# Local and global attention followed by a GELU feed-forward: the last batch's activations are written in output order, its tiles go out in one transfer each, and its last tile is moved to the end

## The chip, the cores and the metric

The kernel runs on one core of one Trainium2 chip. The metric is the device time of one execution in microseconds (us); the median of several runs is compared. The engines are called by the names of the profile: PE (TensorE matmuls; PEld is its weight load), DVE (VectorE), ACT (ScalarE), POOL (GpSimd) and SP (SyncE, which here only issues transfers).

## The reference

The inputs are queries, keys and values for 8 batches with 8 heads of dimension 64: 512 local and 32 global tokens each. Global tokens attend to everything; a local token attends to the global tokens and to the local ones within a window of 32. The result is laid out as tokens by 512 features and goes through a feed-forward of width 2048:

```python
s_g = scale * np.matmul(q_g, k_all.transpose(0, 1, 3, 2))
out_g = np.matmul(sm(s_g), v_all)
mask = np.abs(pos[:, None] - pos[None, :]) <= window      # window = 32
s_l = np.concatenate([s_lg, s_ll], axis=-1)               # s_ll is -1e9 outside the mask
out_l = np.matmul(sm(s_l), np.concatenate([v_g, v_l], axis=2))
x = concat(out_g, out_l): (8 * 544 tokens, 512)
h = x @ w_in                                              # 512 x 2048
g = h * (1.0 / (1.0 + np.exp(-1.702 * h)))
return (g @ w_out).astype(np.float32)                     # 2048 x 512, out is 4352 x 512
```

In the output, the rows of one batch are its 32 global tokens followed by its 512 local ones.

## The kernel before, in words

All matmuls take bf16 operands and accumulate in fp32. The order of the instructions on each engine is the order in which the program writes them; the program interleaves the stages by hand.

The attention works on groups of four heads. It leaves, for each batch, a tile xL of 512 features (four blocks of 128 partitions) by 512 local tokens, and one common tile xG with the 8 x 32 = 256 global tokens. In xL the local tokens are not in output order: token number 16 r + t stands in column 32 t + r (t from 0 to 15, r from 0 to 31). This comes from the way in which queries and keys are loaded, and runs through all later stages.

The feed-forward has two phases for each batch i from 0 to 7, and for i = 8, which the program calls B and which is the set of 256 global tokens:

- The **h phase** has 16 steps, one for each block fc of 128 of the 2048 inner features. `h_step` (L623) takes a PSUM bank hp, does four accumulating matmuls with `h_mm` (L612), and calls `h_act`: a Tanh on ACT from hp into a tile th (L619) and one DVE instruction `(th + 1) * hp` into `gTs[i][:, fc]` in bf16 (L620). A batch has 512 columns, the global tokens have 256. There are four th buffers.
- The **o phase** has one tile `tci` for every 128 tokens: four tiles in a batch, two for the global tokens. `o_mm` (L630) does a quarter of a tile, four accumulating matmuls of 512 columns with gT as the weights (L637); at the fourth quarter `o_out` copies the PSUM bank to the tile ob on ACT with a factor of 0.5 (L651) and issues the output transfers (L659). There are six ob buffers.

hp and op come from one pool of four PSUM banks ("p"), so a new step waits until an earlier one has been read.

A tile of 128 columns holds four values of t, with 32 values of r each. So one output tile of a batch is written by four transfers of 32 rows, and the rows of each lie 16 rows apart in the output. For the global tokens each of the four transfers writes the 32 rows of one batch. All go through SP's queue, apart from the last tile.

The very last tile (`last` in `o_out`; in the kernel before the second tile of the global tokens) is split in its columns, 320 and 192: the 16 matmuls of the first part (L649), the copy and four transfers, then the same for the second part. Its transfers alternate between SP and ACT.

At the end of the program the h phase of the global tokens is interleaved with the o phase of batch 7: one h step, then one quarter of a tile, 16 times. Then come the first tile of the global tokens and the split last tile:

```python
for st in range(FC):
    h_step(B, st)
    o_mm(B - 1, st)
for st in range(4):
    o_mm(B, st)
o_out(B, 1, None)
```

Of the kernel before, what the change touches and what calls it, by code (L numbers as in the profile page):

```python
# [16 lines left out]
ALU = mybir.AluOpType  # L17
# [3 lines left out]
def kernel(  # L21
# [12 lines left out]
    nc = tc.nc  # L34

    B, H, Sl, D = q_l.shape
    Sg = q_g.shape[2]
    S = Sg + Sl
# [123 lines left out]
    for j in range(4):  # L162
        r = (j + 1) % 4
        nc.gpsimd.memset(bd[32 * r : 32 * r + 32, j, :], 1.0)
    for i in range(2):
# [3 lines left out]
        out=step, in_=step, pattern=[[1, 289]], compare_op=ALU.is_ge,  # L169
# [108 lines left out]
    def pbank(name):  # L278
        return psP.tile([128, 512], F32, name=name, tag="p")
# [323 lines left out]
    gTs, ops = {}, {}  # L603

    def width(i):
        return TB if i < B else B * Sg
# [9 lines left out]
    def h_act(i, fc, hp):  # L616
        n = width(i)
        th = moe.tile([128, TB], F32, name="th", bufs=4)
        nc.scalar.activation(th[:, :n], hp[:, :n], AF.Tanh, scale=0.851)  # L619
        nc.vector.scalar_tensor_tensor(gTs[i][:, fc, :n], in0=th[:, :n], scalar=1.0,  # L620
                                       in1=hp[:, :n], op0=ALU.add, op1=ALU.mult)

    def h_step(i, fc):  # L623
        if fc == 0:
            gTs[i] = moe.tile([128, FC, TB], BF16, name="gT")
        hp = pbank("hp")
        h_mm(i, fc, hp, range(NKC))
        h_act(i, fc, hp)

    def o_mm(i, st):  # L630
        tci, f4 = divmod(st, 4)
        first = (i, tci) not in ops
        if first:
            ops[i, tci] = pbank("op")
        op = ops[i, tci]
        for fc in range(4 * f4, 4 * f4 + 4):
            nc.tensor.matmul(op, lhsT=gTs[i][:, fc, tci * 128 : tci * 128 + 128],  # L637
                             rhs=w_out_sb[:, fc, :], start=(first and fc == 4 * f4), stop=(fc == FC - 1))
        if f4 == 3:
            o_out(i, tci, op)  # L640

    def o_out(i, tci, op):
        ob = moe.tile([128, d_model], F32, name="ob", bufs=6)
        last = i == B and tci == B // 4 - 1
        for lo, hi in ((0, 320), (320, 512)) if last else ((0, 512),):
            if last:
                op = pbank("op")
                for fc in range(FC):
                    nc.tensor.matmul(op[:, lo:hi], lhsT=gTs[i][:, fc, tci * 128 : tci * 128 + 128],  # L649
                                     rhs=w_out_sb[:, fc, lo:hi], start=(fc == 0), stop=(fc == FC - 1))  # L650
            nc.scalar.activation(ob[:, lo:hi], op[:, lo:hi], AF.Copy, scale=0.5)  # L651
            for j in range(4):
                eng = nc.scalar if last and j % 2 else nc.sync
                if i < B:
                    rows = out[i * S + Sg : (i + 1) * S, :].rearrange("(r t) m -> t r m", t=16)[4 * tci + j]
                else:
                    r = (4 * tci + j) * S
                    rows = out[r : r + Sg, :]
                eng.dma_start(out=rows[:, lo:hi], in_=ob[32 * j : 32 * j + 32, lo:hi])  # L659

    def act4(i, hf):
        f = slice(2 * hf, 2 * hf + 2)
# [164 lines left out]
    for fc in range(FC):  # L827
        if fc < 4:
            h_act(1, fc, hps[fc])
        elif fc in (4, 6):  # L830
            f = slice(fc, fc + 2)
            th, ps = early[:, fc - 4 : fc - 2], pt[1 - (fc - 4) // 2]
            nc.scalar.activation(th, ps, AF.Tanh, scale=0.851)
            nc.vector.scalar_tensor_tensor(gTs[1][:, f, :], in0=th, scalar=1.0, in1=ps,
                                           op0=ALU.add, op1=ALU.mult)
        elif fc >= 8:
            h_step(1, fc)
        if fc < 4:
            a.ext((fc,), on_act)
        if fc == 10:  # L840
            a.S(0)
            a.X(0, (0,))
        if fc == 11:
            a.X(0, (1,))
            a.M(0, nc.gpsimd)
            load_v(3)
            load(4)
            load_g(8, NQ)
# [72 lines left out]
            phase_o(i)  # L921
    for st in range(FC):
        h_step(B, st)
        o_mm(B - 1, st)
    for st in range(4):
        o_mm(B, st)
    o_out(B, 1, None)


# [28 lines left out]
```

## Time and profile before

| | us |
|---|---|
| median of 3 runs | 299.13 (298.33 to 299.79) |
| profiled execution | 299.75 |
| its span in the profile | 298.0 |
| h phase of batch 7 on PE, about | 252.7 to 266.5 of the span |
| h phase of the global tokens with the o phase of batch 7 | 266.5 to 287.3 |
| last ACT copy (192 columns) | 294.51 to 294.84 |
| last transfers issued | 295.3 |

The profile is that of one execution. Busy times are for one engine; a line number (L620) is a line of the kernel before. Groups are listed as line, engine, operation, output and inputs, shape, count, then busy time in us and mean time of one in ns, then idle time of the engine ahead of them with what ended it. In the timeline a line has start and duration in us, engine, line and operation; several like instructions are merged into one line with their count. "Landing" of a transfer is the time from its issue to its completion.

### The profile page before, as it was taken

The numbers are of one execution on the slowest core, as the hardware profiler recorded it, in microseconds if no ns is written. First come the engines' busy times: TensorE is split into PE (matmuls) and PEld (weight loads), VectorE is DVE, ScalarE is ACT, GpSimd is POOL, SyncE is SP. The second block draws the span as 40 slices with busy tenths as digits, with TensorE's granted clock in tenths as the row PEclk, the third lists the DMA queues.
The fourth block names the chain that finished last, engine by engine and source line by source line (L and its number), as shares of the span: only waits on it lengthen the run. The fifth ranks groups of instructions, "written<-read, shape, count | busy, mean of one in ns | idle before, by whom it ended". The sixth has DMA issues, their size and how long they took to land.

```text
span 298.0 us, 8159 instructions
## 1 busy us (share of the span) xinstructions
PE 287.4 (96%) x3390; PEld 150.2 (50%) x3431; DVE 216.2 (73%) x422; ACT 173.6 (58%) x284; POOL 86.9 (29%) x136
## 2 busy tenths in 40 slices
PE   7999999998999999999999999999999999999995
PEld 6544445444454455445454455445544455445653
DVE  6768868887868878797979878787879766683220
ACT  4836867589347736577357654676547651663421
POOL 8973669639564002800072003500000000000000
PEclk9999999999999999999999999999999999999999
DMA  7999999998999312981199114901120022101113
GB/s 202 166 187 211 204 184 128 187 166 60 163 189 158 72 39 55 144 139 28 48 95 173 34 40 84 113 0 40 36 73 0 2 55 55 35 0 39 36 48 95
DMA packets 59541, 28.20 MB, mean 95 GB/s; under 512 B 47600, under 2 KB 49904, under 8 KB 59504
## 3 DMA queue, kind: packets, MB, share of 16 engines
q0 software_dynamic: 51664, 17.57, 53.5%
q1 hardware_dynamic: 7360, 9.45, 11.6%
q10 hardware_dynamic: 480, 0.66, 0.7%
q8 instruction: 27, 0.44, 0.7%
q14 instruction: 10, 0.08, 0.1%
HBM read 36.31 MB, written 8.91 MB: 152 GB/s over the span
## 4 chain that ended last, share of the span: by engine, by line
PE 86%; DVE 3%; ACT 2%; issue 2%; ACTq 0%; DVEq 0%
PE hp L612 36%; PE op L637 36%; PE s L557 5%; PE ov L583 5%; PE s L612 2%; ACT e L568 2%; ACT ob L651 1%; PE op L649 1%; DVE rs L463 1%; DVE sT L459 1%; DVE xL L468 1%; PE og L594 1%; DVE e L573 0%; PE ov L420 0%; PE ov L435 0%
## 5 line engine op out<-in xcount | busy, mean ns | idle before, releaser
L637 PE MATMUL op<-w_out_sb,gT 128*128 128x512 bf16 x498 | 119.1, 379 | 2.9 <-DVE rs L463 1.2
L620 DVE SCALAR_TENSOR_TENSOR gT<-th,hp 128x512 bf16<-128x512 f32 (+1 forms) x136 | 87.0, 655 | 35.7 <-ACT th L619 35.7
L612 PE MATMUL hp<-xL,w_in_sb 128*128 128x512 bf16 x471 | 104.8, 379 | 0.7 <-issue 0.2
L619 ACT ACTIVATE th<-hp 128x512 f32<-128x512 f32 (+1 forms) x136 | 77.7, 574 | 41.2 <-PE hp L612 38.5
L612 PEld LDWEIGHTS <-w_in_sb 128*128 128x128 bf16 x576 | 56.1, 98 | 64.3 <-issue 0.4
L637 PEld LDWEIGHTS <-gT 128*128 128x128 bf16 x528 | 49.4, 98 | 56.2 <-issue 1.3
L651 ACT ACTIVATE ob<-op 128x512 f32<-128x512 f32 (+2 forms) x35 | 20.5, 589 | 65.9 <-PE op L637 63.3
L97 POOL DMA_DIRECT2D v<-in_v_l_dram x40 | 30.9, 776 | 84.5 <-PE og L594 82.2
L568 ACT ACTIVATE e<-s 128x1016 bf16<-128x1016 f32 (+1 forms) x56 | 53.5, 1007 | 2.9 <-PE s L557 2.8
L573 DVE TENSOR_TENSOR e<-e,mask 128x1712 bf16<-128x1712 bf16 (+1 forms) x26 | 27.5, 1059 | 4.8 <-ACT e L568 4.3
L459 DVE STREAM_TRANSPOSE sT<-ov 128x512 f32<-128x512 f32 x15 | 10.8, 717 | 17.4 <-PE ov L583 15.9
L468 DVE TENSOR_TENSOR xL<-ov,rs 128x512 bf16<-128x512 f32 x29 | 18.7, 686 | 1.8 <-PE ov L435 0.5
L557 PEld LDWEIGHTS <-kT 32*128 32x128 bf16 x672 | 12.7, 93 | 12.5 <-issue 8.8
L509 DVE STREAM_TRANSPOSE kT<-rk 128x512 f32<-128x512 f32 x14 | 14.6, 1044 | 3.1 <-DMA rk<-in_k_l_dram 3.1
L557 PE MATMUL s<-q,kT 32*128 32x160 bf16 (+1 forms) x448 | 14.9, 246 | 0.0
L99 POOL DMA_DIRECT2D v<-in_v_g_dram x24 | 13.9, 581 | 0.2 <-issue 0.2
L463 DVE STREAM_TRANSPOSE rs<-rT 128x512 f32<-128x512 f32 x16 | 11.4, 711 | 0.6
L583 PE MATMUL ov<-e,v 128*32 128x128 bf16 (+3 forms) x624 | 11.7, 223 | 0.0
L314 DVE STREAM_TRANSPOSE q<-rq 128x512 f32<-128x512 f32 (+1 forms) x17 | 11.3, 665 | 0.2 <-ACT rq L675 0.2
L583 PEld LDWEIGHTS <-v 128*32 128x32 bf16 x672 | 10.5, 97 | 0.0
L612 PE MATMUL hp<-xG,w_in_sb 128*128 128x256 bf16 x64 | 9.6, 273 | 0.0
L557 PE MATMUL s<-qc,kT 32*128 32x120 bf16 (+1 forms) x224 | 8.0, 212 | 0.2 <-ACT e L568 0.2
(109 smaller groups left out, 182.4 us busy)
## 6 DMA issues: line engine op xcount, KB each, us to landing
out_dram<-ob SPq DMA_DIRECT2D x132, 64.0 KB, 2.3
rq<-in_q_l_dram POOLq DMA_DIRECT2D x5, 512.0 KB, 7.2
rk<-in_k_l_dram POOLq DMA_DIRECT2D x5, 512.0 KB, 9.9
v<-in_v_l_dram POOLq DMA_DIRECT2D x24, 96.0 KB, 4.2
w_in_sb<-in_moe_w_in_dram POOLq DMA_DIRECT2D x8, 256.0 KB, 7.8
w_out_sb<-in_moe_w_out_dram POOLq DMA_DIRECT2D x4, 512.0 KB, 10.3
rq<-in_q_l_dram POOLq DMA_DIRECT2D x5, 256.0 KB, 6.5
rk<-in_k_l_dram POOLq DMA_DIRECT2D x5, 256.0 KB, 7.7
```

The source lines that it names most:

```text
L97: nc.gpsimd.dma_start(out=vt[0:n, hs, c, :D], in_=vs[FIRST[c] : FIRST[c] + n, hs])
L468: nc.vector.tensor_mul(self.x[:, 2 * self.u + h, :], self.st[1 + h], self.st["rs"])
L509: nc.vector.transpose(flat[:, 0:Sl].rearrange("p (r t) -> p t r", t=16), loaded[self.b][0][:, self.u].bitcast(F32))
L557: nc.tensor.matmul(bank(self.ps, j)[:, at : at + n], lhsT=self.k[p, KEYS[c] : KEYS[c] + 128, e], rhs=qs[p, :, :, e], start=(e == 0), stop= ...
L568: nc.scalar.activation(self.E[rnd][:, 2 * i : 2 * i + 2, :n], self.ps[i][:, :, :n], AF.Exp, scale=scale)
L573: eng.tensor_mul(e, e, mask[:, rnd : rnd + 1, :n].to_broadcast([128, 4, n]))
L583: nc.tensor.matmul(ov[32 * j : 32 * j + 32, :].rearrange("p (t r) -> p t r", t=16)[:, t0:t1, r0 : r0 + nr], lhsT=lv, rhs=self.E[rnd][:, j, ...
L612: nc.tensor.matmul(hp[:, : width(i)], lhsT=w_in_c[:, fc // 4, kc, fc % 4 // 2, :, fc % 2], rhs=(xL[i] if i < B else xG)[:, kc, :], start=( ...
L619: nc.scalar.activation(th[:, :n], hp[:, :n], AF.Tanh, scale=0.851)
L620: nc.vector.scalar_tensor_tensor(gTs[i][:, fc, :n], in0=th[:, :n], scalar=1.0, in1=hp[:, :n], op0=ALU.add, op1=ALU.mult)
L637: nc.tensor.matmul(op, lhsT=gTs[i][:, fc, tci * 128 : tci * 128 + 128], rhs=w_out_sb[:, fc, :], start=(first and fc == 4 * f4), stop=(fc = ...
L651: nc.scalar.activation(ob[:, lo:hi], op[:, lo:hi], AF.Copy, scale=0.5)
```

## The change

Three things are changed, all of them for batch 7 and the end of the program.

First, `h_act` writes batch 7's gT in output order. Inputs th and hp are read in sequence as before; the output is addressed so that column 32 t + r of the input goes to column 16 r + t. Successive bf16 results therefore go 16 elements (32 bytes) apart.

Second, in `o_out` a tile of batch 7 now consists of 128 rows that follow each other in the output, and goes out in one transfer through SP instead of four. The global tokens keep four transfers a tile, all on SP.

Third, the order at the end: the first four h steps of the global tokens follow each other without an `o_mm`; the other twelve are each followed by one quarter of tiles 0, 1 and 2 of batch 7. Then come both tiles of the global tokens, unsplit, and at the very end the last tile of batch 7, split 320 and 192, with one transfer for each part.

```diff
@@ h_act
-        nc.vector.scalar_tensor_tensor(gTs[i][:, fc, :n], in0=th[:, :n], scalar=1.0,
-                                       in1=hp[:, :n], op0=ALU.add, op1=ALU.mult)
+        g, th, hp = gTs[i][:, fc, :n], th[:, :n], hp[:, :n]
+        if i == B - 1:
+            g = g.rearrange("p (r t) -> p t r", t=16)
+            th, hp = (v.rearrange("p (t r) -> p t r", t=16) for v in (th, hp))
+        nc.vector.scalar_tensor_tensor(g, in0=th, scalar=1.0, in1=hp, op0=ALU.add, op1=ALU.mult)
@@ o_out
-        last = i == B and tci == B // 4 - 1
+        last = i == B - 1 and tci == 3
...
             nc.scalar.activation(ob[:, lo:hi], op[:, lo:hi], AF.Copy, scale=0.5)
+            if i == B - 1:
+                r = i * S + Sg + 128 * tci
+                nc.sync.dma_start(out=out[r : r + 128, lo:hi], in_=ob[:, lo:hi])
+                continue
             for j in range(4):
-                eng = nc.scalar if last and j % 2 else nc.sync
...
-                eng.dma_start(out=rows[:, lo:hi], in_=ob[32 * j : 32 * j + 32, lo:hi])
+                nc.sync.dma_start(out=rows[:, lo:hi], in_=ob[32 * j : 32 * j + 32, lo:hi])
@@ the end
     for st in range(FC):
         h_step(B, st)
-        o_mm(B - 1, st)
-    for st in range(4):
+        if st >= 4:
+            o_mm(B - 1, st - 4)
+    for st in range(8):
         o_mm(B, st)
-    o_out(B, 1, None)
+    o_out(B - 1, 3, None)
```

## The prediction

> **What bounds the kernel now.** I read the page first, then the chain of waits at its end, then the timeline of the last 45 us, and last the groups of DVE instructions with their shapes kept apart. The page's first line:
>
> ```profile
> PE 287.4 (96%) x3390; PEld 150.2 (50%) x3431; DVE 216.2 (73%) x422; ACT 173.6 (58%) x284; POOL 86.9 (29%) x136
> ```
>
> TensorE is busy for 96% of the span and its granted clock is full in all 40 slices, so time is lost only where PE is made to stop, or behind its last matmul. The timeline of the stretch that the change touches:
>
> ```profile
> 254.40 0.69 DVE L620 SCALAR_TENSOR_TENSOR gT<-th,hp 128x512 bf16<-128x512 f32 x1 [2.98 <-ACT th L619]
> 254.65 12.03 PE L612 MATMUL hp<-xL,w_in_sb 128*128 128x512 bf16 x54
> ...
> 266.49 0.69 DVE L620 SCALAR_TENSOR_TENSOR gT<-th,hp 128x512 bf16<-128x512 f32 x1 [0.17 <-ACT th L619]
> 266.52 0.60 PE L612 MATMUL hp<-xG,w_in_sb 128*128 128x256 bf16 x4
> ...
> 267.35 1.02 DVE L620 SCALAR_TENSOR_TENSOR gT<-th,hp 128x512 bf16<-128x512 f32 x2 [0.18 <-ACT th L619]
> ```
>
> The h phase of batch 7 starts its 16 DVE instructions at 254.40 to 267.35, so one step lasts (267.35 - 254.40)/15 = 0.863 us, and that is PE's pace: each DVE instruction takes 0.69 us and then sits idle 0.17 us, waiting for ACT, which waits for PE. DVE has 0.17 us of cover in each step. At 266.52 PE goes on with the global tokens (256 columns). The end of the chain:
>
> ```profile
> 286.67 4.26 PE op L637 x19
> 290.94 2.19 PE op L649 x16
> 293.15 0.45 ACT ob L651
> ```
>
> From here PE, one ACT copy and the last output transfers follow each other.
>
> **DVE: the new write order (the term that decides).** The 16 instructions of batch 7 keep their element count (the built program has them as 128x16x32), but each bf16 result now lands 32 bytes behind the one before. No row of before shows this instruction with such a step. The nearest rows:
>
> ```profile
> L620 DVE SCALAR_TENSOR_TENSOR gT<-th,hp 128x512 bf16<-128x512 f32 x120 | 80.3, 686 | 22.9 <-ACT th L619 22.9
> L509 DVE STREAM_TRANSPOSE kT<-rk 128x512 f32<-128x512 f32 x14 | 14.6, 1044 | 3.1 <-DMA rk<-in_k_l_dram 3.1
> L314 DVE STREAM_TRANSPOSE q<-rq 128x512 f32<-128x512 f32 x15 | 10.5, 697 | 0.0
> L310 DVE STREAM_TRANSPOSE kT<-rk 128x256 f32<-128x256 f32 x2 | 1.2, 608 | 0.0
> L314 DVE STREAM_TRANSPOSE q<-rq 128x256 f32<-128x256 f32 x2 | 0.8, 422 | 0.2 <-ACT rq L675 0.2
> ```
>
> L509 and L310 write kT through the view "p (r t) -> p t r", a step of 64 bytes; L314 writes the same number of elements in sequence. Strided: (1044 - 608)/256 = 1.70 ns an element; in sequence: (697 - 422)/256 = 1.07. For 512 elements the step costs 512 x 0.63 = 0.32 us by the slopes, 1044 - 697 = 0.35 us by the means. Added to 0.69 us: I take 1.03 us for one instruction. The Trainium skill, in "SBUF — State Buffer", section "Door 1: The DMA port swizzle (why `[64,N]` ≈ `[32,N]`)", speaks against this change too: an access that crosses to a new 16-byte line pays a penalty; by that rule every one of the new writes pays, and the kT rows agree with 0.35 us in 512, though the page has no figure.
>
> What counts is the spacing of such instructions back to back, since their ends overlap:
>
> ```profile
> 227.01 3.15 DVE L620 SCALAR_TENSOR_TENSOR gT<-th,hp 128x512 bf16<-128x512 f32 x5
> ...
> 34.85 1.00 DVE L509 STREAM_TRANSPOSE kT<-rk 128x512 f32<-128x512 f32 x1
> 35.71 0.66 DVE L314 STREAM_TRANSPOSE q<-rq 128x512 f32<-128x512 f32 x1
> ```
>
> Five contiguous ones took 3.15 us: spacing (3.15 - 0.69)/4 = 0.615. With the step that becomes 0.615 + 0.32 to 0.35 = 0.94 to 0.96. The pair at 34.85 has a strided instruction followed after 0.86 us, 0.14 less than its duration, which would make 1.03 - 0.14 = 0.89. I take 0.93. That is over PE's 0.863, so DVE falls behind by 0.07 us in every step of batch 7. The other price ends: none at all (spacing 0.615; the instruction handles the same elements, so a gain is excluded), and twice the contiguous price of an element (about 1.035 ns, from 686 ns here and 421 ns for 128x256): 0.69 + 0.53 = 1.22 us, spacing 0.615 + 0.53 = 1.145.
>
> **Who waits for it, and the four steps without o_mm.** Each hp of the h phase and each op of the output phase takes one of four PSUM banks ("p"). PE's first matmul into a bank waits until DVE has read the step four before. The changed loop issues h_step(B, 0..3) back to back, 0.44 us of PE each, where before an o_mm of 0.86 us lay behind each; so step 3 of the global tokens, free of waits, would start at 266.52 + 3 x 0.44 = 267.84. It waits for DVE's step 15 of batch 7. That ends at
>
> 254.40 + 15 x 0.93 + 1.03 = 269.38 us,
>
> and with 0.03 us for the semaphore (the gap from PE's end to the ACT copy at 293.15) PE starts it at 269.41: 1.57 us late. The same sum with in-sequence writes: 267.35 + 0.69 + 0.03 = 268.07, late by 0.23, which is the price of the reordering alone. Small stalls from fc 13 on are inside the 1.57, because it is counted to an absolute moment. If o_mm stayed between the h steps, 3 x 0.86 us of PE work would cover it. Behind step 3 nothing more is lost: from step 4 each turn has 0.44 + 0.86 = 1.30 us of PE against 0.42 us of DVE and at most 0.39 + 0.60 us of ACT. The three o_mm tiles in 12 turns and the whole tiles at the end contain the same matmuls as before (4 tiles of batch 7, 2 of global tokens, one of the six split 320/192), so PE's sum is unchanged and the delay goes through to the end undiminished. ACT's th has four buffers and waits for DVE four steps back, later in the step than PE's bank: it adds nothing.
>
> **Output transfers.** Batch 7 issues 3 + 2 transfers instead of 16, and the tile that now comes second to last keeps four on SP, instead of eight pieces on SP and ACT: 11 issues less on SP, 4 less on ACT (about 0.4 us each). None but the last lies on the path, and SP and ACT have idle time around them; the ob buffers are six tiles deep, and no ACT wait on a transfer shows in this stretch. At the end:
>
> ```profile
> 295.80:295.90 0.10, 0.00 (x0) 0.00 (x0) 0.00 (x0) 0.00 (x0) 0.00 (x0) 1.00 0.86 223
> ...
> 296.20:296.30 0.10, 0.00 (x0) 0.00 (x0) 0.00 (x0) 0.00 (x0) 0.00 (x0) 1.00 0.73 192
> ...
> out_dram<-ob SPq DMA_DIRECT2D x2, 24.0 KB, 1.4
> out_dram<-ob ACTq DMA_DIRECT2D x2, 24.0 KB, 1.6
> ```
>
> The last two columns of the windows are the busy share of the 16 DMA engines and GB/s. The second 192-column pair, issued at 295.30, moves its bytes 0.4 us behind the first, and lands at about 295.30 + 1.6 = 296.9. One transfer of 96 KB issued at 294.88 saves that second issue (0.42 us), but carries four times the rows: at one pair's 0.35 us for 48 KB it needs 0.7 us, lands about 296.7 and gains 0.2; if the rows spread as the 128-row loads at 4 us do (384 to 405 GB/s, 0.25 us), it lands about 296.35 and gains 0.55. I take 0.3, and 0.2 of loss as the other end (descriptors of 128 rows made in one go). The Trainium skill (same page and section) says that partitions 0 to 63 reach 8 of 16 ports and 128 reach all; by that rule the gain would be the 0.55 and the sum 0.25 us lower.
>
> **Sum.** +1.57 - 0.3 = +1.3 us. The profiled execution took 299.75 us (span 298.0 and 1.75 around it) and would take 301.0; it lies 0.62 above the median of the runs, so for the median 299.13 + 1.3 = 300.4 us, 0.4% more. With spacings of 0.89 and 1.03 and the gain's ends the forecast's own range is 299.6 to 302.4.
>
> **Rivals.**
> *The write is hidden (not slower).* For: a bf16 row with a 32-byte step, in its reading, is cheaper than kT's: the mask bias (L203, 192 elements) took 408 ns, (408 - 156)/192 = 1.31 ns with the 156 ns that L620's two sizes leave as fixed. That makes 0.83 us and a spacing of 0.75, under 0.863, and then only the step-3 wait of 0.23 to 0.38 is lost. Against: it is a read. It decides if the spacing stays under 0.863. With the end's gain of 0.3 to 0.55: 298.8 to 299.2, say 299.1.
> *A two-byte strided write is dearer than a four-byte one.* For: nothing here shows that size written apart; against: kT's slope at a wider step. At 1.145 spacing: 254.40 + 17.18 + 1.22 + 0.03 - 267.84 = +4.99, less 0.3: 303.8.
> *The last transfer of 128 rows lands late.* The first 128-row loads took 3.9 to 4.8 us to land, but among much other traffic; at 2.8 us, the longest landing of the last ten us, the end is lost by 0.8 us in place of won by 0.3: 301.5.
> That the change is not done as said I exclude: the built streams show the 128x16x32 form, the 128-row transfers and four h steps in a row.
>
> **Chances.** Forecast 0.55, hidden write 0.22, dearer write 0.18, late landing 0.05. The range of 298.8 to 303.6 leaves out most of the dearer case and a little below. About 0.5% (1.5 us) is what a measurement of this kernel can tell from no change. The forecast lies just under it and splits evenly: 0.27 slower, 0.28 same. Slower: 0.27 + 0.18 + 0.03 = 0.48. Same: 0.28 + 0.17 + 0.02 = 0.47. Faster: 0.05, from the hidden write alone, with a gain that no row above prices.
>
> **What would show it.** The 128x512 group of the changed line at about 1.03 us for 16 instructions, back to back with no idle time at the end of batch 7; a PE wait for DVE of some 1.5 us in total, most of it in the first four steps of 256 columns; PE's last matmul later by as much; the last landing 0.2 to 0.5 us nearer to the last ACT copy. Wrong, if these instructions stay near 0.7 us, if PE shows no gap there, or if they exceed 1.15 us.

## The result, and the profile after

The changed kernel takes 322.5 us (median of 6 runs, 321.84 to 323.39) against 299.05 for the kernel before in the same runs: 7.8% more, ratio 1.078 with a 95% interval of 1.075 to 1.081. The profiled execution took 322.04 us with a span of 320.3.

The change kept every matmul and the loss is almost all in one group. Groups of DVE, with the shapes kept apart (busy time, mean ns of one, idle time before):

```profile
L624 DVE SCALAR_TENSOR_TENSOR gT<-th,hp 128x512 bf16<-128x512 f32 x120 | 104.0, 933 | 20.3 <-ACT th L619 20.3
```

L624 is L620 of before. The 104 instructions of this form ahead of batch 7 are as they were (686 ns, within 1), so the 16 of batch 7 have a mean of (120 x 933 - 104 x 686)/16 = 2.54 us: 3.7 times as long, not the 1.03 us of the forecast. The chain that ended last (start, duration, engine, tile, line):

```profile
253.46 34.72 DVE gT L624 x16
288.18 0.04 issue
288.22 1.87 PE hp L612 x8
290.09 1.71 PE op L640 x4
291.79 0.85 PE hp L612 x4
292.65 0.99 PE op L640 x4
293.64 0.44 PE hp L612 x4
...
305.78 7.77 PE op L640 x36
313.55 3.51 PE op L652 x32
317.05 0.02 issue
317.08 0.33 ACT ob L654
```

The chain of before ran through PE in this stretch:

```profile
259.40 7.72 PE hp L612 x37
267.12 0.86 PE op L637 x4
```

It now runs through DVE for 34.72 us without a break: a spacing of (34.72 - 2.55)/15 = 2.145 us where PE needs 0.863. PE's own timeline shows the other side of it, one step of four matmuls and then a wait:

```profile
258.03 1.02 PE L612 MATMUL hp<-xL,w_in_sb 128*128 128x512 bf16 x4 [1.15 <-DVE gT L624]
260.19 1.02 PE L612 MATMUL hp<-xL,w_in_sb 128*128 128x512 bf16 x4 [1.13 <-DVE gT L624]
```

At 288.22 step 3 of the global tokens starts, released by DVE as the prediction described. The matmuls behind it are slow at first: an o_mm quarter takes 1.71 and 0.99 us where it took 0.86. Windows of that time (length, busy time of PE, PEld, DVE, ACT and POOL, granted clock, DMA share, GB/s):

```profile
276.00:280.00 4.00, 1.73 (x8) 0.62 (x7) 4.00 (x3) 1.19 (x2) 0.00 (x0) 1.00 0.00 0
...
284.00:288.00 4.00, 1.53 (x8) 0.86 (x8) 4.00 (x3) 0.77 (x2) 0.00 (x0) 0.74 0.00 0
288.00:292.00 4.00, 3.78 (x14) 2.08 (x14) 1.91 (x6) 0.77 (x2) 0.00 (x0) 0.50 0.02 4
```

PE has 0.863 us of work in each 2.145 us, 40%; at 288 to 292 its clock is granted at half.

The sum, counted from the first DVE instruction of batch 7 (254.40 before, 253.46 after) to the end of the span: 43.60 us before, 66.84 after, +23.24. By the prediction's count step 3, in the new order and free of waits, would start 13.44 us behind that instruction (at 267.84 on the clock of before); it starts 34.76 us behind it (288.22): +21.32. From there to 293.48, five pieces of 0.44, 0.44, 0.86, 0.44 and 0.86 us take 5.26 in place of 3.04: +2.22, the clock. The end gives back 0.27: from the last ACT copy to the end of the span 2.89 us in place of 3.16. Together that is +23.27, against the +23.24 of the spans.

### The profile page after: what moved, and what is told of

Its sections match the earlier page's. It is cut to its first block, busy times and chain, and to the rows that moved or that the text cites. A ratio compares the mean times of both kernels' runs of the same rounds, so it can differ in the third digit from the quotient of the medians.

```text
span 320.3 us, 8183 instructions
## 1 busy us (share of the span) xinstructions
PE 298.0 (93%) x3431; PEld 151.8 (47%) x3431; DVE 239.1 (75%) x422; ACT 173.5 (54%) x284; POOL 86.9 (27%) x136
## 4 chain that ended last, share of the span: by engine, by line
PE 78%; DVE 13%; ACT 2%; issue 1%; ACTq 0%; DVEq 0%
PE op L640 34%; PE hp L612 30%; DVE gT L624 11%; PE s L557 5%; PE ov L583 4%; PE s L612 2%; ACT e L568 1%; PE op L652 1%; DVE sT L459 1%; DVE xL L468 1%; ACT ob L654 1%; PE og L594 1%; DVE rs L463 0%; DVE e L573 0%; PE ov L420 0%
## 5 line engine op out<-in xcount | busy, mean ns | idle before, releaser
L624 DVE SCALAR_TENSOR_TENSOR gT<-th,hp 128x512 bf16<-128x512 f32 (+1 forms) x136 | 110.3, 875 | 32.4 <-ACT th L619 32.4
L640 PE MATMUL op<-w_out_sb,gT 128*128 128x512 bf16 x528 | 122.0, 382 | 0.6 <-DVE rT L461 0.6
L612 PE MATMUL hp<-xL,w_in_sb 128*128 128x512 bf16 x480 | 110.1, 386 | 10.4 <-DVE gT L624 10.2
L612 PEld LDWEIGHTS <-w_in_sb 128*128 128x128 bf16 x576 | 57.2, 100 | 84.9 <-issue 24.4
L557 PEld LDWEIGHTS <-kT 32*128 32x128 bf16 x672 | 12.7, 93 | 12.5 <-issue 8.8
L612 PE MATMUL hp<-xG,w_in_sb 128*128 128x256 bf16 x64 | 11.1, 308 | 5.4 <-DVE gT L624 5.4
```

The lines of the kernel that those rows point to most:

```text
L557: nc.tensor.matmul(bank(self.ps, j)[:, at : at + n], lhsT=self.k[p, KEYS[c] : KEYS[c] + 128, e], rhs=qs[p, :, :, e], start=(e == 0), stop= ...
L612: nc.tensor.matmul(hp[:, : width(i)], lhsT=w_in_c[:, fc // 4, kc, fc % 4 // 2, :, fc % 2], rhs=(xL[i] if i < B else xG)[:, kc, :], start=( ...
L624: nc.vector.scalar_tensor_tensor(g, in0=th, scalar=1.0, in1=hp, op0=ALU.add, op1=ALU.mult)
```

## The experiments

The theory after the result: a bf16 result that is written apart from its neighbour, so that only half of a 4-byte word is written, is much dearer than an fp32 one, whatever lies around it. Rivals: the step of 32 bytes, the folded reading of PSUM, contention with ACT and PE, and the order at the end.

### The disputed instruction by itself

A kernel of its own, with variants like these, five or three of each:

```diff
+    def stt(g, a, b):
+        nc.vector.scalar_tensor_tensor(g, in0=a, scalar=1.0, in1=b, op0=ALU.add, op1=ALU.mult)
+    # bf_32B: results 16 bf16 elements apart; other sets have other steps, and fp32
+    stt(t[:, k].rearrange("p (r t) -> p t r", t=16), fold(th, 16), fold(hp, 16))
+    # run_of_two: two results beside each other, every 32 bytes
+    stt(t[:, k, :, 0:2], th.rearrange("p (a e) -> p a e", e=2), hp.rearrange("p (a e) -> p a e", e=2))
```

> This kernel computes none of the reference: it fills the output with zeros and runs the disputed DVE instruction by itself, 512 results a partition, with PE idle, in sets of five that differ in the size of a result (bf16 or fp32), in the step between results (2 to 64 bytes) and in the second input (PSUM or SBUF), then some copies on DVE and ACT. Theory two-byte: a bf16 result written apart from its neighbours costs about 4 clocks whatever the step above some line, an fp32 one about 1.7; then bf_32B and bf_64B take 2.3 to 2.6 us, fp_32B and fp_64B 1.0 to 1.1, and runs of two bf16 results fall to about half. Theory step: 32 bytes is a worse step than 64; then fp_32B is as dear as bf_32B (2.2 or more) and bf_64B is near 1.03. Theory PSUM or shape: the folded reading of hp is at fault; then sb_bf_32B is near 1.03 and all folded sets are dear. Theory contention: other engines slow the write in the full kernel; then bf_32B is near 1.03 here.

The timeline of DVE; the number behind bf_ or fp_ is the step in bytes, and a set's spacing is the distance to the start of the next set divided by its count:

```profile
4.10 3.06 DVE L65 SCALAR_TENSOR_TENSOR bf_2B<-th,hp 128x512 bf16<-128x512 f32 x5
7.08 3.12 DVE L65 SCALAR_TENSOR_TENSOR bf_4B<-th,hp 128x512 bf16<-128x512 f32 x5
10.11 5.80 DVE L65 SCALAR_TENSOR_TENSOR bf_8B<-th,hp 128x512 bf16<-128x512 f32 x5
15.72 11.52 DVE L65 SCALAR_TENSOR_TENSOR bf_16B<-th,hp 128x512 bf16<-128x512 f32 x5
26.88 11.04 DVE L65 SCALAR_TENSOR_TENSOR bf_32B<-th,hp 128x512 bf16<-128x512 f32 x5
37.56 11.45 DVE L65 SCALAR_TENSOR_TENSOR bf_64B<-th,hp 128x512 bf16<-128x512 f32 x5
48.65 3.26 DVE L65 SCALAR_TENSOR_TENSOR fp_4B<-th,hp 128x512 f32<-128x512 f32 x5
51.83 3.07 DVE L65 SCALAR_TENSOR_TENSOR fp_8B<-th,hp 128x512 f32<-128x512 f32 x5
54.82 4.67 DVE L65 SCALAR_TENSOR_TENSOR fp_16B<-th,hp 128x512 f32<-128x512 f32 x5
59.33 4.75 DVE L65 SCALAR_TENSOR_TENSOR fp_32B<-th,hp 128x512 f32<-128x512 f32 x5
63.92 4.46 DVE L65 SCALAR_TENSOR_TENSOR fp_64B<-th,hp 128x512 f32<-128x512 f32 x5
...
70.61 10.89 DVE L65 SCALAR_TENSOR_TENSOR sb_bf_32B<-th,h 128x512 bf16<-128x512 f32 x5
81.13 4.78 DVE L65 SCALAR_TENSOR_TENSOR rd_both<-th,hp 128x512 bf16<-128x512 f32 x5
85.83 1.86 DVE L65 SCALAR_TENSOR_TENSOR run_of_two<-th,hp 128x512 bf16<-128x512 f32 x3
87.62 1.87 DVE L65 SCALAR_TENSOR_TENSOR run_of_four<-th,hp 128x512 bf16<-128x512 f32 x3
...
91.21 1.08 DVE L103 COPY cp_bf_2B<-b 128x512 bf16<-128x512 bf16 x5
92.22 5.63 DVE L105 COPY cp_bf_32B<-b 128x512 bf16<-128x512 bf16 x5
```

| | spacing of one, us | per visit to a 16-byte line, ns |
|---|---|---|
| bf16 in sequence; 4 bytes apart | 0.60; 0.61 | not the limit |
| bf16 8 bytes apart | 1.12 | 4.4 |
| bf16 16, 32, 64 bytes apart | 2.23, 2.14, 2.22 | 4.2 to 4.4 |
| the same at 32 bytes, both inputs in SBUF | 2.10 | 4.1 |
| fp32 8 bytes apart | 0.60 | not the limit |
| fp32 16, 32, 64 bytes apart | 0.90, 0.92, 0.86 | 1.7 to 1.8 |
| two bf16 beside each other, every 32 bytes | 0.60 | at most 2.3 |

The price alone, 2.14 us, is that of the changed kernel (2.145): contention has no part in it. The step is not it either: 16, 32 and 64 bytes cost alike. PSUM is not it (2.10 from SBUF). The size is: fp32 results at the same 32 bytes take 0.92 us. And the size alone is not enough: two bf16 results that fill a word cost nothing extra, while two per line that each fill half a word (8 bytes apart) cost 4.4 ns a line. Nor is every half-filled word dear: 4 bytes apart, with four results in each 16-byte line, 128 lines at 4.4 ns would be 0.56 us, less than the 0.60 that the instruction takes in sequence anyway, and 0.61 was measured. So the price goes by the visit to a line of 16 bytes (it stops rising at that step), and it is higher where the results leave words half filled. The theory had expected runs of two at about half the price; they were free.

This price is that of the disputed instruction, with its fp32 inputs. The last set, a copy of bf16 to bf16 within SBUF with the same step of 32 bytes, took (5.63 - 1.447)/4 = 1.05 us each with the 1.447 us of one, 2.0 ns a line, against 0.20 in sequence: lone bf16 results are not equally dear in every instruction. Whether the type of the input or the instruction makes that difference, and why a half-filled word is dearer at all, no run here shows.

### An fp32 result in the full kernel

```diff
+    wide = []
...
+            if fc == 0:
+                nc.gpsimd.memset(gTs[i], 0.0)
+                wide.append(moe.tile([128, 2, TB], F32, name="wide", bufs=1))
-            g = g.rearrange("p (r t) -> p t r", t=16)
+            g = wide[0][:, fc % 2, :].rearrange("p (r t) -> p t r", t=16)
```

> The changed kernel, but batch 7's DVE instruction writes fp32 results 64 bytes apart into a spare tile, and gT of batch 7 is zeros from POOL: the results of batch 7 are left out, the instructions and their order stay. Theory half-words: the price of the change is that of lone 2-byte results, an fp32 result costs what it does alone (0.86 to 0.92 us spacing, as in kT's row), and the time is that of read_steps, 300 to 301. Rival, in the full kernel (ACT and PE reading SBUF beside it) any write with a wide step is that slow: 322.

Measured 300.03 us, ratio to before 1.001 (0.998 to 1.004). In its DVE timeline:

```profile
253.68 14.15 DVE L629 SCALAR_TENSOR_TENSOR wide<-th,hp 128x512 f32<-128x512 f32 x16 [2.97 <-ACT th L621]
```

One takes 1.046 us (the median of the 16; the forecast had 1.03), their spacing is (14.15 - 1.05)/15 = 0.873. The same instructions at the same places, with results of twice the width and so 64 bytes apart in place of 32 (two steps that cost alike above), take 14.15 us in place of 34.72. The rival of a slow write in the full kernel falls. The spacing is close to the 0.863 of PE, so DVE hardly falls behind: step 3 starts 267.88 - 253.68 = 14.20 us behind the first DVE instruction, 0.76 later than free of waits.

### Reading apart in place of writing apart

```diff
-            g = g.rearrange("p (r t) -> p t r", t=16)
-            th, hp = (v.rearrange("p (t r) -> p t r", t=16) for v in (th, hp))
+            g = g.rearrange("p (r t) -> p r t", t=16)
+            th, hp = (v.rearrange("p (t r) -> p r t", t=16) for v in (th, hp))
```

> The whole change, but the DVE instruction writes gT in sequence and reads th (SBUF) and hp (PSUM) 128 bytes apart. Theory any access off a line costs alike: spacing 2.16 us, 322. Theory only two-byte writes are that dear and fp32 steps cost as in kT's row: 1.03 us an instruction, spacing 0.93, 300.4. Theory reading apart is free: 0.69 us, 299.1.

Measured 301.38 us, ratio 1.005 (1.002 to 1.008): the second theory, and with a spacing of 0.95 us close to what the prediction had drawn. Its chain:

```profile
254.57 15.35 DVE gT L624 x16
269.96 1.03 PE hp L612 x8
```

Step 3 starts 15.39 us behind the first DVE instruction, 1.95 later than free of waits; the prediction's sum at this kernel's spacing (15.35 - 1.06)/15 = 0.953 is 15 x 0.953 + 1.06 + 0.03 - 13.44 = 1.95. The delay goes through to the end: from the first DVE instruction to the last ACT copy it took 42.02 us, 1.91 more than the 40.11 of before. So the path of the sum holds; for the change its price was wrong.

### The order alone, and the queue at the end

Batch 7 in sequence with four transfers a tile, in the changed order:

```diff
-        if i == B - 1:
-            g = g.rearrange("p (r t) -> p t r", t=16)
-            th, hp = (v.rearrange("p (t r) -> p t r", t=16) for v in (th, hp))
...
-            if i == B - 1:
-                r = i * S + Sg + 128 * tci
-                nc.sync.dma_start(out=out[r : r + 128, lo:hi], in_=ob[:, lo:hi])
-                continue
```

> The changed order at the end alone: batch 7's gT is written in sequence and its tiles keep four transfers each, all on SP. By my sum: the four h steps back to back cost 0.23 us at step 3, and the last tile's four SP issues in a row of 0.37 us each, in place of two on SP and two on ACT, cost about 0.7 us: +0.9 us, 300 us. Theory write step is all: the same, within 0.5% of before. Rival, the order is what is dear: 310 us or more, with PE waiting in the four steps.

Measured 300.8 us, ratio 1.005 (1.003 to 1.008). From the first DVE instruction of batch 7 to the last ACT copy it took 40.32 us, before 40.11: the 0.2 us of step 3, which starts 13.69 us behind that instruction, 0.25 later than free of waits. From the end of that copy (293.45) to the end of the span (298.2) it took 4.75 us against 3.16. SP's queue shows why:

```profile
290.25 5.57 SPq L658 DMA_DIRECT2D out_dram<-ob  x12
```

Twelve issues without a pause, up to 295.82, 2.4 us behind the last copy. The cost, 1.59 us, is twice the 0.7 that was expected, because the four issues of the tile ahead stood in the same queue. To test this, the eight pieces were split over SP and ACT again:

```diff
-                nc.sync.dma_start(out=rows[:, lo:hi], in_=ob[32 * j : 32 * j + 32, lo:hi])
+                eng = nc.scalar if last and j % 2 else nc.sync
+                eng.dma_start(out=rows[:, lo:hi], in_=ob[32 * j : 32 * j + 32, lo:hi])
```

> order_only with one thing changed: the split last tile's eight pieces alternate between SP and ACT as before. Theory: of order_only's 1.8 us, 0.25 is the wait at step 3 and 1.6 is SP's queue of twelve issues of 0.42 us behind the last copies; with half of the last eight on ACT about 0.8 to 1.2 comes back, because eight pieces of the tile ahead still stand in SP's queue: 299.4. Rival, SP's queue is not what is late: 300.8 as in order_only.

Measured 299.93 us, ratio 1.000 (0.997 to 1.003); from the copy's end to the span's end 297.8 - 294.56 = 3.24 us. All of the 1.5 us came back, more than expected. In the changed kernel the single transfers have the same effect with fewer issues.

### The order of before with the strided write

```diff
...
     for st in range(FC):
         h_step(B, st)
-        if st >= 4:
-            o_mm(B - 1, st - 4)
-    for st in range(8):
+        o_mm(B - 1, st)
+    for st in range(4):
         o_mm(B, st)
-    o_out(B - 1, 3, None)
+    o_out(B, 1, None)
```

The last tile is again the second one of the global tokens, with its pieces on SP and ACT.

> The strided write and the single transfers of batch 7, but the order of before: one o_mm quarter behind each h step of the global tokens, and the last tile that of the global tokens, eight transfers. Theory: DVE still takes 16 x 2.16 us, PE waits for it in the h phase as much as in the changed kernel, and three quarters of 0.86 us are done in the waits of steps 0 to 2, so 2.6 us less than the changed kernel, and 0.3 more at the end: about 320. Rival, the missing quarters are what makes the wait: near 301.

Measured 319.93 us, ratio 1.068 (1.062 to 1.074): as the theory had it. The moved o_mm quarters are worth some 2.6 us of the 23 (322.5 - 319.93); the wait itself stays.

### PE kept busy in its waits

```diff
+        n = (4 if fc > 4 else 0) if i == B - 1 else 6 if i == B and fc < 4 else 0
...
+            for _ in range(n):
+                nc.tensor.matmul(spare[0][:, 0, :], lhsT=warm[:, 0:128], rhs=warm, start=True, stop=True)
         hp = pbank("hp")
```

> The changed kernel with matmuls of zeros into a spare PSUM bank in front of batch 7's steps 5 to 15 (four each, 0.86 us at full clock) and of the first four global steps (six each, 1.3 us), where PE otherwise waits for DVE; their result is used by nothing. DVE sets the pace at 2.16 us a step, so they fit in the waits. Theory idle: PE's waits are what lowers its granted clock, and the low clock behind them costs the last 2.2 us of the loss; then the clock stays at 1.0 and the time falls by 1.5 to 2.5 us, to about 320.5. Rival: the clock falls for another reason, or the loss at the slow stretch is not from the clock: 322.5 or more.

Measured 320.01 us, ratio 1.070 (1.066 to 1.075) against the change's 1.078; granted clock 1.0 throughout. From the first DVE instruction to the last copy 61.67 us in place of 63.62: 1.95 less with more work for PE. Step 3 starts 35.04 us behind the first DVE instruction, 0.28 later than in the changed kernel, so the stretch behind it is 2.23 us shorter: the 2.22 of the sum. With the waits filled the low clock is gone, and with it these 2.2 us.

### Ways to put the permutation elsewhere

Three kernels put it where DVE writes in sequence, with the o_mm quarters behind the first twelve global steps:

```diff
-        if st >= 4:
-            o_mm(B - 1, st - 4)
+        if st < 12:
+            o_mm(B - 1, st)
@@ pe_read_early: PE reads xL apart
+            if i == B - 1:
+                x = x.rearrange("p (t r) -> p r t", t=16)
...
@@ pe_write_early: PE writes hp apart
+            if i == B - 1:
+                h = h.rearrange("p (r t) -> p t r", t=16)
...
```

> The permutation is moved to PE's moving operand: batch 7's h matmuls read xL 64 bytes apart, so that hp, th and gT are in output order and ACT and DVE work in sequence; single transfers as in the change; the o_mm quarters behind the first twelve global steps. Theory PE reads apart for nothing: the end's gain alone, 0.3 us under before. Rival, PE pays for a new line as DVE does when it reads (0.34 us in 512): 64 matmuls, +22 us, 321.

> As pe_read_early, but PE reads xL in sequence and writes its fp32 results into PSUM 64 bytes apart. Theory PSUM takes them for nothing: 0.3 us under before. Rival, PSUM charges a new line as SBUF charges DVE for fp32 results (0.3 us in 512): +19 us or more.

Both rivals were right in kind: 341.18 us (ratio 1.142, 1.137 to 1.146), 42 us more where 22 were expected, and 311.79 us (1.043, 1.040 to 1.046), 12.5 more where 19 were. The groups of PE in the h phase of batch 7, of pe_read_early and pe_write_early:

```profile
L615 PE MATMUL hp<-xL,w_in_sb 128*128 128x512 bf16 x56 | 48.2, 1036 | 0.0
```

```profile
L615 PE MATMUL hp<-xL,w_in_sb 128*128 128x512 bf16 x63 | 27.4, 633 | 0.2 <-issue 0.2
```

A matmul of 512 columns costs 48.2/56 = 0.86 us of PE when it reads bf16 64 bytes apart, 27.4/63 = 0.43 when it writes fp32 to PSUM 64 bytes apart, and 0.216 (0.863/4) in sequence. With the strided read the granted clock fell to 0.5 after some 3.7 us and stayed there to the end of the phase, with no idle time of PE between its instructions; with the strided write it stayed at 1.0. The 0.86 us is the read and not the clock: the weight loads, one ahead of each matmul, start at 251.04, 251.89, 252.74 and 253.60, while the clock is still granted in full (to 254.6), and 0.86 us apart in the same way behind that, at 0.5.

The third was to be read_steps with better cover:

> Like read_steps (DVE writes gT in sequence and reads its inputs 128 bytes apart, spacing 0.955 us there), but the o_mm quarters of tiles 0 to 2 stand behind the first twelve global steps instead of the last twelve. Theory cover: a DVE that is 1.5 us behind at the end of the h phase is caught up behind three quarters of 0.86 us, and of read_steps' loss only some 0.4 us is left, against a gain at the end of 0.3: 299.3. Rival, the lag goes through whatever lies between: 300.8 as in read_steps.

As run, DVE both reads and writes in sequence: this kernel leaves the reordering out (batch 7's rows land in other places) and says nothing on the theory. It shows what the single transfers and the new last tile are worth when the permutation costs nothing, with the o_mm quarters in this place: 298.85 us, ratio 0.999 (0.996 to 1.001), no measurable gain. In its trace the first DVE instruction to the last copy takes 40.07 us (before 40.11), and the end behind that copy is 0.24 us shorter. With the reordering in:

> What read_early was meant to be: DVE writes in sequence and reads 128 bytes apart (0.955 us spacing), the o_mm quarters behind the first twelve global steps, single transfers. Theory cover: of read_steps' 1.9 us at step 3 about 0.4 is left, with 0.3 gained at the end, within 0.3 us of before: 299.3. Rival, no cover: 300.8.

Measured 300.38 us, ratio 1.003 (1.000 to 1.007). From the first DVE instruction to the last copy 41.09 us: 0.98 more than before, half of read_steps' 1.91. Cover is real, but less than expected, because the first o_mm takes a bank of the same four and waits too. It starts 269.18 - 255.68 = 13.50 us behind the first DVE instruction, before 266.96 - 254.40 = 12.56, and these 0.94 us are nearly all of the 0.98:

```profile
268.24 0.60 PE L612 MATMUL hp<-xG,w_in_sb 128*128 128x256 bf16 x4
269.18 1.02 PE L640 MATMUL op<-w_out_sb,gT 128*128 128x512 bf16 x4 [0.35 <-DVE gT L624]
```

No version was measurably faster than the kernel before.

## Why the prediction was wrong

**The step that failed is the price of one DVE instruction.** The prediction took 1.03 us for a duration and 0.93 for the spacing; they were 2.54 and 2.145. It borrowed the price from a strided write of kT, a transpose with fp32 elements. The measurement by itself shows that this price is about right for fp32 (0.86 to 0.92 us spacing, and 1.046 us for one in the full kernel) and does not carry over to bf16. The rival of a dearer two-byte write named the mechanism with a chance of 0.18, but its bound of twice the contiguous price, 1.22 us, had no row behind it and was half of what came: no row of before shows a half-word written apart, and the range should have said so by being open at that end.

**The path held.** With the measured spacing the same formula gives 15 x 2.145 + 2.55 + 0.03 - 13.44 = 21.32 us for step 3, which is the +21.32 of the trace. It also gives read_steps (1.95 for 1.95). PE's bank four steps back, the four h steps in a row and the absence of anything later that waits were right. Its aside that o_mm between the h steps would cover the lag held only in part: in read_cover half of it was left, because the first o_mm waits for a bank itself. The price of the reordering alone, 0.23, is the 0.2 of order_only.

**One term was missing.** The prediction counted waiting as time lost and no more. PE with 40% of work for 30 us lost its clock at times, and 2.2 us went behind the wait. At the forecast's spacing of 0.93 it would hardly have been there: in read_steps, with a spacing of 0.953 and step 3 late by 1.95 us, the mean clock is 0.999.

**The end was right.** 0.3 us of gain were forecast and 0.27 came. The 0.3 was chosen between 0.2 and 0.55 without a row to decide between them, so that it came this near is in part luck. The second issue (0.42 us) is gone, and the one transfer of 96 KB lands after 1.7 us where the pieces of 24 KB took 1.4 to 1.6. Its bytes move at 253 to 338 GB/s where the pairs had 192 to 223:

```profile
318.30:318.40 0.10, 0.00 (x0) 0.00 (x0) 0.00 (x0) 0.00 (x0) 0.00 (x0) 1.00 0.74 253
318.40:318.50 0.10, 0.00 (x0) 0.00 (x0) 0.00 (x0) 0.00 (x0) 0.00 (x0) 1.00 1.01 338
```

The Trainium skill's rule of 8 ports for partitions 0 to 63 and 16 for all 128 ("SBUF — State Buffer", "Door 1: The DMA port swizzle (why `[64,N]` ≈ `[32,N]`)") agrees with these rates; the gain of 0.55 us that the prediction worked out by it did not come. The hidden write and the late landing did not occur (the first 128-row loads, by the rows, landed after 3.7 to 4.9 us and not 3.9 to 4.8; nothing hangs on it).

## What to carry to other kernels

Price a strided write by the width of its element as well as by its step: in the instruction measured here bf16 results 16 bytes or more apart took 3.6 times the spacing of the same results in sequence (8 bytes apart 1.9 times, 4 bytes apart no more), and fp32 ones about 1.4 times. If a permutation has to be made in bf16, let the engine read apart and write in sequence (0.94 us by itself, with fp32 inputs), or write in pairs (0.60 us, measured by itself only), and look at what the permutation buys first: here the shorter end was worth some 0.3 us in the traces and nothing measurable in the medians. Where one engine becomes the pace, follow the last released step to an absolute time, and add what PE's clock loses while it waits.

## What the runs showed of the hardware

- DVE's results cost 4.1 to 4.4 ns for each visit to a 16-byte line where they are bf16 and leave words half filled, 1.7 to 1.8 where they are fp32, and at most 2.3 where two bf16 results fill a word, all in scalar_tensor_tensor with fp32 inputs; a copy of bf16 to bf16 paid 2.0 ns for a lone result. The same section of the Trainium skill's "SBUF — State Buffer" says that up to 8 bf16 elements (16 bytes) of stride are free; here 2 elements were free, 4 cost 1.12 us and 8 cost 2.23 against 0.60. For fp32 it says 4 elements; here a step of 2 was free and 4 already cost 0.90.
- ScalarE pays about the same as that instruction. Its copies of 512 columns in the kernel of variants, in sequence, as bf16 32 bytes apart and as fp32 64 bytes apart:

```profile
91.32 2.56 ACT L108 ACTIVATE act_bf_2B<-hp 128x512 bf16<-128x512 f32 x5 [89.31 <-DVE run_of_eight L65]
93.72 10.97 ACT L110 ACTIVATE act_bf_32B<-hp 128x512 bf16<-128x512 f32 x5
104.21 4.74 ACT L112 ACTIVATE act_fp_64B<-hp 128x512 f32<-128x512 f32 x5
```

  That is 0.48, 2.10 and 0.91 us each ((93.72 - 91.32)/5, (104.21 - 93.72)/5, and (4.74 - 1.105)/4 with the duration of one).
- The granted clock fell to 0.5 although PE was never idle for more than 1.6 us at a time. The Trainium skill, "TensorE: Matmul & The Clock Gate", "Part 1: The HAM clock gate (the "warmup" mystery)", has the clock fall after an idle window of about 3.4 us; here a busy share of 40% in steps of 2.15 us was enough, and filling the waits kept it at 1.0. In pe_read_early it fell to 0.5 with no idle time in PE's record at all, while each matmul took 0.86 us in place of 0.216.
- The same instructions ahead of batch 7 took from 252.80 us (order_only) to 255.68 us (read_cover) up to its first DVE instruction in these profiles. Effects of some 0.3 us could only be read by counting from that instruction.
